# Softmax steps listed at other tiles, and additions right behind their products, in a fused window-sum and max-out kernel

## The chip, the cores and the metric

The kernel runs on one core of one Trainium2 chip. The metric is the time of one execution on the device, in microseconds; of several executions the median is given.

## What is computed

The reference has two parts. The first takes, for each position, a softmax over seven taps and sums the seven most recent rows of `x` with it, per head (8 heads of 24 columns; 8 sequences of 4160 positions):

```python
w = weight_gen - np.max(weight_gen, axis=-1, keepdims=True)
w = np.exp(w)
w = w / (np.sum(w, axis=-1, keepdims=True) + 1e-09)
...
out = np.einsum('bshk,bskhg->bshg', w, x_unf)
```

The second part takes the 33280 rows of 192 values that come out and applies two matrices of 192 x 1024, the larger of the two results, and a matrix of 1024 x 192:

```python
h1 = x @ w1
h2 = x @ w2
g = np.maximum(h1, h2)
return (g @ w_out).astype(np.float32)
```

Inputs and output are float32.

## The kernel before

**Layout.** A partition holds 260 consecutive positions. They are cut into 17 batches: 16 of 16 positions and one of 4. A batch is done in halves of 8 positions (quarters of 4 in the first two batches). In the second part a *tile* is 1/8 of the hidden units for the 8 positions of one half (1024 tokens), so there are as many tiles as positions, 260: batch `b` needs its first half at tile 16b and its second at tile 16b+8.

**Per half on VectorE.** `mul` (L164, the product itself at L173) multiplies the seven shifted copies of `x` with the weights. `adds` (L179) adds the seven products in three steps (L189, L195, L198); the last writes `y_t`. Between these, in the argument `beside`, stand pieces of other batches' softmax: `shift` (L144, three pieces), which subtracts the logarithm of the sum from the exponents of the next batch, and `red` (L135, two pieces), which sums the exponentials of a batch further on. All batches share one product tile `m_t`.

**Per batch on ScalarE.** The softmax has three steps there: `exp_sum` (L125, L127) takes the exponentials to be summed, `ln` (L141) the logarithm of the sums, and `weights` (L150, L158) the exponentials of the shifted exponents, per half; these are the weights that `mul` reads. So for batch `c` the order is `exp_sum`, `red`, `ln`, `shift`, `weights`, `mul`, `adds`, with the engine changing at nearly every step.

**Transposes.** SyncE issues a DMA transpose of each finished half of `y_t` into `yt` (L207), in one queue with the stores of the results (L383). `transpose` also lets GpSimd wait for the landing by a one-column copy (L215) and then issue the loads of `x` (L115) and of `weight_gen` (L105) of later batches.

**TensorE and its other engine.** Since max(a, b) = a + relu(b - a), TensorE computes `hd` = x(w2 - w1) (L275), ScalarE applies relu into `rd_t` (L285), and TensorE adds the rest: `op_ps` from `yt` and `w10` = w1 w_out (L327), then from `rd_t` and `wo` (L315). ScalarE copies the results out (L371). This goes by *groups* of three tiles (two before tile 16). In each group `hidden` (L434) lists: the first matmuls of the group's first tiles, the results of earlier tiles (first halves), the relu of the first tiles, the group's last tile, its relu, the second halves of the results, and the copies out. A group computes two results or four. `OUTS` fixes which; from tile 58 on they alternate, before that two groups of two results often follow one another.

**Where the softmax steps stand.** Each engine works through its queue in the order in which the program lists the instructions; nothing is reordered. In a group with two results the softmax steps of ScalarE are listed after the copies out, in a group with four between the relu of the first two tiles and that of the last one (`beside`). Which steps those are is decided by the table `due` (L677 to L687): for each batch and step a tile number. `softmax_steps` (L690) takes what has become due in the tiles of the group; a long step (`weights`, `exp_sum`) that becomes due in a group with four results is put off to the next group, if the group with two results just before it had a long step. `extra` (L703) lists VectorE's work and the transposes by the tile's place `s` in its batch.

Of the kernel before, what the change touches and what calls it, by code (L numbers as in the profile page):

```python
# [17 lines left out]
def _sub(base: bass.AP, off: int, dims):  # L18
    ap = [list(base.ap[0])] + [[int(s), int(c)] for s, c in dims]
    return dataclasses.replace(base, offset=base.offset + off, ap=ap)  # L20
# [3 lines left out]
def kernel(  # L24
# [25 lines left out]
    NB = len(BATCHES)  # L50


    def pieces(b):
        n = BATCHES[b][1]
        at, done = [], 0
        for w in (4, 4, 4, 4) if b < 2 else (8, 8) if n == 16 else (n,):
            at.append((done, w))
            done += w
        return at
# [65 lines left out]
    def exp_sum(b):  # L125
        e_ts[b] = pe_.tile([P, BATCHES[b][1] * WGC], FP32, name="e_t", tag="e")
        nc.scalar.activation(out=e_ts[b], in_=wg_ts[b], func=AF.Exp)  # L127
# [7 lines left out]
    def red(b, i=0, of=1):  # L135
        if i == 0:
            s_ts[b] = psm.tile([P, BATCHES[b][1] * H], FP32, name="sum_t", tag="sum")
        hs, at, ap = part(b, i, of)
        nc.vector.reduce_sum(out=s_ts[b][:, hs], in_=_sub(e_ts[b], at, ap), axis=AX.X)  # L139

    def ln(b):  # L141
        nc.scalar.activation(out=s_ts[b], in_=s_ts[b], func=AF.Ln)  # L142

    def shift(b, i=0, of=1):  # L144
        hs, at, ap = part(b, i, of)
        w_t = _sub(wg_ts[b], at, ap)
        nc.vector.tensor_tensor(out=w_t, in0=w_t, in1=_sub(s_ts[b], hs.start, [[1, hs.stop - hs.start], [0, K]]),  # L147
                                op=ALU.subtract)

    def weights(b, o):  # L150

        w = dict(pieces(b))[o]
        if b not in en_ts:
            en_ts[b] = pen.tile([P, 16 * WGC * 2], BF16, name="en_t", tag="en")
        J = 2 if w == 4 and b < 2 else 1
        N = w * H // J
        for j in range(J):
            nc.scalar.activation(  # L158
                out=_sub(en_ts[b], (o * WGC + j * N * K) * 2, [[2 * N, K], [2, N], [1, 2]]),
                in_=_sub(wg_ts[b], (o * H + j * N) * K, [[1, K], [K, N], [0, 2]]), func=AF.Exp,  # L160
            )


    def mul(b, o):  # L164

        n = dict(pieces(b))[o]
        if n == 4 and b < 2:
            m_out = _sub(m_t, K * o * D, [[64, 2], [P, K * 6], [1, 64]])
            x_in = _sub(xb_ts[b], o * D, [[2 * D, 2], [D, K], [1, 2 * D]])
        else:  # L170
            m_out = m_t[:, K * o * D:K * (o + n) * D]
            x_in = _sub(xb_ts[b], o * D, [[D, K], [1, n * D]])
        nc.vector.tensor_tensor(  # L173
            out=m_out, in0=x_in,
            in1=_sub(en_ts[b], o * WGC * 2, [[2, K * n * H], [0, G // 2], [1, 2]]),
            op=ALU.mult,
        )

    def adds(b, o, first=False, beside=lambda i, of: None):  # L179


        w = dict(pieces(b))[o]
        n = w * D

        def taps(at, step, cnt):
            return _sub(m_t, K * o * D + at * n, [[step * n, cnt], [1, w * D]])

        beside(0, 3)
        nc.vector.tensor_tensor(out=taps(0, 1, 3), in0=taps(0, 1, 3), in1=taps(3, 1, 3), op=ALU.add)  # L189
        if first:  # L190
            return
        beside(1, 3)
        if b not in y_ts:
            y_ts[b] = py.tile([P, 16 * D], BF16, name="y_t", tag="y")
        nc.vector.tensor_tensor(out=taps(0, 2, 2), in0=taps(0, 2, 2), in1=taps(1, 5, 2), op=ALU.add)  # L195
        beside(2, 3)

        nc.vector.tensor_tensor(  # L198
            out=_sub(y_ts[b], o * D, [[64, 2], [P, 3 * w // 2], [1, 64]]),
            in0=taps(0, 1, 1), in1=taps(2, 1, 1), op=ALU.add,  # L200
        )

    def transpose(u):

        b, o, n = UNITS[u]
        yt = pyt.tile([P, 8 // 2 * 3 * P], BF16, name="yt", tag="yt")
        nc.sync.dma_start_transpose(  # L207
            out=yt[:, 0:n // 2 * 3 * P].rearrange("p (b t) -> p b t", t=P),
            in_=y_ts[b][:, o * D:(o + n) * D],
        )  # L210
        yt_ts[u] = yt
        while held:
            held.pop(0)()

        nc.gpsimd.tensor_copy(out=gate, in_=yt[:, 0:1])  # L215
        c = b + 1 if o == 0 else b + 2
        if o == 8 and c < NB:
            load_x(c, 0, min(8, BATCHES[c][1]))
        if o == 0 and c < NB and BATCHES[c][1] > 8:
            load_x(c, 8, BATCHES[c][1] - 8)  # L220
        if o == 0 and b + 3 < NB:
            load_wg(b + 3, nc.gpsimd)
# [179 lines left out]
    OUTS, c = [[], [], []], 0  # L402
# [274 lines left out]
    due = {}  # L677
    for c in range(3, NB):
        soon = c < 5
        parts_ = [(16 * (c - 2) + (8 if soon else 12), True, lambda c=c: weights(c, 0))]  # L680
        if 8 in dict(pieces(c)):
            parts_.append((16 * (c - 2) + (14 if soon else 17), True, lambda c=c: weights(c, 8)))
        if c > 3:
            parts_.append((16 * (c - 2) + (0 if c < 10 else 2 if c < 14 else 4), False, lambda c=c: ln(c)))
            parts_.append((16 * (c - 3) + (4 if c < 6 else 8), True, lambda c=c: exp_sum(c)))
        for t, *step in parts_:
            due.setdefault(t, []).append(step)  # L687
    waiting, long_in_two = [], [False]
# [14 lines left out]
    def extra(t):  # L703

        u, k = TILES[t]
        b, o, n = UNITS[u]
        s = o + k

        if s == 0 and b + 1 < NB:
            mul(b + 1, 0)  # L710
        if s == 5 and b + 1 < NB:

            c = b + 1
            adds(c, 0, beside=lambda i, of: shift(c + 1, i, of) if c + 1 < NB else None)
        if s == 8 and b + 2 < NB:
            mul(b + 1, 8)
        if s == 13 and b + 2 < NB:
            adds(b + 1, 8, beside=lambda i, of: red(b + 3, i, 2) if b + 3 < NB and i < 2 else None)
        if k == n // 4 - 1 and 7 < u + 1 < NU:
            transpose(u + 1)  # L720

    def steps(g, tiles):

        if tiles:
            softmax_steps(g)
        for t in tiles:
            extra(t)
# [47 lines left out]
```

## Time and profile before

| | us |
|---|---|
| median of 6 runs | 420.38 |
| lowest, highest | 419.48, 422.0 |
| the profiled execution | 419.53 |
| its span, first to last instruction | 417.7 |
| busy: TensorE matmuls, VectorE, ScalarE, GpSimd | 396.4, 377.4, 359.3, 84.6 |
| one `mul` of a half (L173, 128x10752) | 5.75 |
| the three additions (L189, L195, L198) of a half | 2.55, 1.75, 0.95 |
| one `weights` of a half or `exp_sum` of a batch on ScalarE | 1.04, 0.95 |
| one `ln` | 0.33 |
| DMA transpose, issue to landing: least, median, most | 3.6, 3.7, 8.1 |

A profile line of the timeline reads: start, length, engine, line of the kernel, operation, what it writes and reads, number of instructions merged; in brackets the time that the engine stood idle before it, and who ended that. A line of the waits reads: who waited, for whom, microseconds in total, number of times, the longest. A matmul's end in these rows is modelled and overlaps the next, so the pace of TensorE is read from the starts. The granted clock of TensorE is 0.997 of full speed over the span.

### The profile page before, as it was taken

The numbers are of one execution on the slowest core, as the hardware profiler recorded it, in microseconds if no ns is written. First come the engines' busy times: TensorE is split into PE (matmuls) and PEld (weight loads), VectorE is DVE, ScalarE is ACT, GpSimd is POOL, SyncE is SP. The second block draws the span as 40 slices with busy tenths as digits, with TensorE's granted clock in tenths as the row PEclk, the third lists the DMA queues.
The fourth block names the chain that finished last, engine by engine and source line by source line (L and its number), as shares of the span: only waits on it lengthen the run. The fifth ranks groups of instructions, "written<-read, shape, count | busy, mean of one in ns | idle before, by whom it ended". The sixth has DMA issues, their size and how long they took to land.

```text
span 417.7 us, 16033 instructions
## 1 busy us (share of the span) xinstructions
PE 396.4 (95%) x7369; PEld 320.5 (77%) x7369; DVE 377.4 (90%) x218; ACT 359.3 (86%) x424; POOL 84.6 (20%) x102
## 2 busy tenths in 40 slices
PE   7769899989999999899999999999999999999995
PEld 7668799767777777677787777877777777777795
DVE  5999999799989989999999999999999999999100
ACT  5888998789988999788999899999898998987871
POOL 1510101452313142011222122112121221121000
PEclk9999999999999999999999999999999999999998
DMA  8965425679864954786497677569759737742613
GB/s 246 262 159 165 107 78 79 153 135 248 169 134 80 260 134 93 226 206 137 78 264 180 85 234 175 122 140 224 157 121 218 182 66 215 189 88 78 210 53 139
DMA packets 60242, 65.68 MB, mean 157 GB/s; under 512 B 47601, under 2 KB 48497, under 8 KB 60176
## 3 DMA queue, kind: packets, MB, share of 16 engines
q1 hardware_dynamic: 51904, 40.47, 35.8%
q0 software_dynamic: 8128, 24.11, 28.5%
q8 instruction: 57, 0.93, 0.9%
q14 instruction: 9, 0.07, 0.1%
q10 hardware_dynamic: 144, 0.10, 0.1%
HBM read 35.96 MB, written 25.56 MB: 147 GB/s over the span
## 4 chain that ended last, share of the span: by engine, by line
PE 56%; DVE 23%; ACT 11%; issue 5%; DMA 3%; SPq 1%; ACTq 0%; DVEq 0%
PE op_ps L315 26%; PE hd L275 25%; DVE m_t L173 11%; ACT rd_t L285 6%; PE op_ps L327 5%; DVE m_t L189 5%; DVE m_t L195 3%; ACT en_t L158 2%; DMA ws1T<-in_moe_w_dram 2%; DVE sum_t L139 1%; DMA yt<-y_t 1%; DVE y_t L198 1%; DVE wg_t L147 1%; ACT o_t L371 1%; ACT yt L246 1%
## 5 line engine op out<-in xcount | busy, mean ns | idle before, releaser
L285 ACT ACTIVATE rd_t<-hd 128x1024 bf16<-128x1024 f32 (+1 forms) x206 | 234.4, 1186 | 29.0 <-PE hd L275 27.7
L315 PE MATMUL op_ps<-wo,rd_t 64*128 64x192 bf16 x4160 | 210.5, 243 | 0.2
L315 PEld LDWEIGHTS <-rd_t 64*128 64x128 bf16 x4160 | 180.3, 94 | 16.1 <-ACTq L348 0.9
L173 DVE TENSOR_TENSOR m_t<-xb_t,en_t 128x10752 bf16<-128x10752 bf16 (+1 forms) x37 | 187.5, 5071 | 3.6 <-ACT en_t L158 3.5
L275 PE MATMUL hd<-yt,wd 64*128 64x512 bf16 (+1 forms) x1584 | 187.5, 360 | 3.0 <-ACT rd_t L285 2.3
L275 PEld LDWEIGHTS <-wd 64*128 64x128 bf16 x1776 | 94.2, 94 | 46.6 <-issue 5.7
L215 POOL CAST gate<-yt 128x1 f32<-128x1 bf16 x29 | 48.6, 1676 | 270.8 <-DMA yt<-y_t 270.8
L189 DVE TENSOR_TENSOR m_t<-m_t 128x4608 bf16<-128x4608 bf16 (+1 forms) x34 | 79.5, 2339 | 0.1
L371 ACT COPY o_t<-op_ps 128x384 f32<-128x384 f32 (+1 forms) x99 | 57.0, 586 | 12.4 <-PE op_ps L315 12.3
L327 PE MATMUL op_ps<-w,yt 64*128 64x192 bf16 x780 | 55.4, 243 | 5.2 <-ACT w L628 1.8
L327 PEld LDWEIGHTS <-yt 64*128 64x128 bf16 x780 | 38.3, 94 | 22.3 <-issue 7.2
L195 DVE TENSOR_TENSOR m_t<-m_t 128x3072 bf16<-128x3072 bf16 (+1 forms) x29 | 50.0, 1723 | 0.1
L158 ACT ACTIVATE en_t<-wg_t 128x896 bf16<-128x896 f32 (+2 forms) x45 | 34.9, 816 | 0.1
L198 DVE TENSOR_TENSOR y_t<-m_t 128x1536 bf16<-128x1536 bf16 (+1 forms) x29 | 27.3, 941 | 0.5
L147 DVE TENSOR_TENSOR wg_t<-wg_t,sum_t 128x280 f32<-128x280 f32 (+4 forms) x45 | 22.0, 489 | 3.0 <-ACT sum_t L142 3.0
L361 DVE COPY o_t<-op_ps 128x192 f32<-128x192 f32 x1 | 0.4, 358 | 25.5 <-ACT o_t L361 25.5
L115 POOL DMA_DIRECT2D xb_t<-in_x_dram x32 | 17.3, 540 | 23.8 <-DVE m_t L173 15.8
L139 DVE TENSOR_REDUCE sum_t<-e_t 128x64 f32<-128x448 f32 (+2 forms) x30 | 19.5, 650 | 2.6 <-ACT e_t L127 2.6
L127 ACT ACTIVATE e_t<-wg_t 128x896 f32<-128x896 f32 (+1 forms) x17 | 15.9, 936 | 4.2 <-DMA wg_t<-in_weight_gen_dram 4.2
L285 ACT ACTIVATE rd_t<-hdp 128x1024 bf16<-128x1024 f32 x16 | 15.9, 1028 | 1.2 <-PE hdp L275 1.0
L275 PE MATMUL hdp<-yt,wd 64*128 64x256 bf16 x192 | 13.1, 269 | 2.2 <-ACT yt L246 1.1
L590 PE MATMUL warm<-ident 128*128 128x128 bf16 x129 | 8.8, 238 | 3.0 <-DVE ident L529 3.0
(45 smaller groups left out, 79.5 us busy)
## 6 DMA issues: line engine op xcount, KB each, us to landing
out_dram<-o_t SPq DMA_DIRECT2D x28, 768.0 KB, 5.1
xb_t<-in_x_dram POOLq DMA_DIRECT2D x28, 384.0 KB, 5.0
wg_t<-in_weight_gen_dram POOLq DMA_DIRECT2D x14, 448.0 KB, 6.1
xb_t<-xb_t POOLq DMA_DIRECT2D x16, 288.0 KB, 5.2
out_dram<-o_t SPq DMA_DIRECT2D x8, 384.0 KB, 2.7
wg_t<-in_weight_gen_dram SPq DMA_DIRECT2D x2, 448.0 KB, 5.4
xs<-in_x_dram SPq DMA_DIRECT2D x2, 384.0 KB, 6.4
xb_t<-in_x_dram POOLq DMA_DIRECT2D x1, 768.0 KB, 7.2
```

The source lines that it names most:

```text
L147: nc.vector.tensor_tensor(out=w_t, in0=w_t, in1=_sub(s_ts[b], hs.start, [[1, hs.stop - hs.start], [0, K]]), op=ALU.subtract)
L158: nc.scalar.activation(out=_sub(en_ts[b], (o * WGC + j * N * K) * 2, [[2 * N, K], [2, N], [1, 2]]), in_=_sub(wg_ts[b], (o * H + j * N) * K ...
L173: nc.vector.tensor_tensor(out=m_out, in0=x_in, in1=_sub(en_ts[b], o * WGC * 2, [[2, K * n * H], [0, G // 2], [1, 2]]), op=ALU.mult,)
L189: nc.vector.tensor_tensor(out=taps(0, 1, 3), in0=taps(0, 1, 3), in1=taps(3, 1, 3), op=ALU.add)
L195: nc.vector.tensor_tensor(out=taps(0, 2, 2), in0=taps(0, 2, 2), in1=taps(1, 5, 2), op=ALU.add)
L198: nc.vector.tensor_tensor(out=_sub(y_ts[b], o * D, [[64, 2], [P, 3 * w // 2], [1, 64]]), in0=taps(0, 1, 1), in1=taps(2, 1, 1), op=ALU.add,)
L215: nc.gpsimd.tensor_copy(out=gate, in_=yt[:, 0:1])
L275: nc.tensor.matmul(hid_out(t, f, j), lhsT=wd[half(j), s * F + f * P:s * F + (f + 1) * P], rhs=_sub(yt_ts[u][half(j), :], (s + j) % 3 * P, ...
L285: nc.scalar.activation(out=rd[:, k * 1024:(k + n) * 1024], in_=hd[:, at:at + n * 1024], func=AF.Relu)
L315: return nc.tensor.matmul(op_out(c), lhsT=rd[half(r), k * 1024 + at:k * 1024 + at + P], rhs=wo[half(r), f * D:(f + 1) * D], start=False, s ...
L327: nc.tensor.matmul(op_out(c + j), lhsT=yt_ts[u][half(j), (3 * i + (s + j) % 3) * P:(3 * i + (s + j) % 3 + 1) * P], rhs=w10[half(j), s * D: ...
L371: nc.scalar.copy(out=_sub(o, c % 24 * D, [[D, len(qs)], [h * D, 2], [1, D]]), in_=_sub(tile_, at + (qs[0] - p) * D, [[D, len(qs)], [512, 2 ...
```

## The change

The tile numbers in the table `due` are changed, and with them the place of each softmax step of ScalarE:

- `weights` of the first half, from batch 5: two tiles earlier; of the second half: two tiles earlier,
- `ln`: batch 4 two tiles earlier; batches 8 and 9 two tiles later, batches 11 to 13 two tiles later; the others stay,
- `exp_sum`: batch 5 three tiles later, batches 6 to 16 one tile earlier.

Since a group takes three tiles, and long steps can be put off, a step moves by a whole number of groups: some do not move, and some that keep their tile number do. Of those that move: `weights` of batch 4 (first half) goes from the group of tiles 40-42 to 43-45, `exp_sum` of batch 5 from 34-36 to 37-39, `ln` of batch 4 from 31-33 to 28-30, `weights` of batch 6 (first half) from 79-81 to 73-75, `ln` of batch 8 from 94-96 to 97-99, `weights` of batch 16 from 235-237 to 232-234. Both halves of `weights` stand in one group for batches 6, 9, 12 and 15 before, and for batches 5, 8, 11 and 14 after.

In addition the three additions of a half, with their `beside` pieces, are listed at the tile of their product for the first batches (`later` is 0 up to b = 3), and five tiles after it as until now for the rest.

```diff
-        parts_ = [(16 * (c - 2) + (8 if soon else 12), True, lambda c=c: weights(c, 0))]
+        parts_ = [(16 * (c - 2) + (8 if soon else 10), True, lambda c=c: weights(c, 0))]
         if 8 in dict(pieces(c)):
-            parts_.append((16 * (c - 2) + (14 if soon else 17), True, lambda c=c: weights(c, 8)))
+            parts_.append((16 * (c - 2) + (14 if soon else 15), True, lambda c=c: weights(c, 8)))
         if c > 3:
-            parts_.append((16 * (c - 2) + (0 if c < 10 else 2 if c < 14 else 4), False, lambda c=c: ln(c)))
-            parts_.append((16 * (c - 3) + (4 if c < 6 else 8), True, lambda c=c: exp_sum(c)))
+            ln_at = -2 if c == 4 else 0 if c < 8 else 2 if c < 11 else 4
+            parts_.append((16 * (c - 2) + ln_at, False, lambda c=c: ln(c)))
+            parts_.append((16 * (c - 3) + (4 if c == 4 else 7), True, lambda c=c: exp_sum(c)))
...
-        if s == 5 and b + 1 < NB:
+        later = 0 if b < 4 else 5
+        if s == later and b + 1 < NB:
 
             c = b + 1
             adds(c, 0, beside=lambda i, of: shift(c + 1, i, of) if c + 1 < NB else None)
         if s == 8 and b + 2 < NB:
             mul(b + 1, 8)
-        if s == 13 and b + 2 < NB:
+        if s == 8 + later and b + 2 < NB:
             adds(b + 1, 8, beside=lambda i, of: red(b + 3, i, 2) if b + 3 < NB and i < 2 else None)
```

## The prediction

> **Names.** Groups go by their tiles ("group 43-45"); a wide group computes four results, a narrow one two. W(c,o) is `weights`, L(c) `ln`, E(c) `exp_sum` (ScalarE); M(c,o) `mul`, S(c) the three `shift` pieces, R(c) the two `red` pieces (VectorE). All times are us of the profiled execution; "before" is the kernel as profiled.
>
> **What bounds the kernel now.** I read the page's busy times first, then the waits in total, then the timeline at each TensorE wait.
>
> ```profile
> PE 396.4 (95%) x7369; PEld 320.5 (77%) x7369; DVE 377.4 (90%) x218; ACT 359.3 (86%) x424; POOL 84.6 (20%) x102
> ```
> ```profile
> ACT sum_t L142 <- DVE sum_t L139: 5.3, 4, 1.8
> ...
> DVE m_t L173 <- ACT en_t L158: 3.5, 3, 2.1
> ...
> DVE wg_t L147 <- ACT sum_t L142: 3.0, 3, 2.2
> ...
> PE hd L275 <- ACT rd_t L285: 2.3, 2, 1.8
> ```
>
> Three engines are nearly full, so I took the pace of two of them from the timeline. TensorE: from a group's first L327 matmul to the next group's it is 5.08 after a wide and 3.56 after a narrow group, so 8.64 per six tiles or 23.0 per batch of 16. VectorE: M(10,0) starts at 242.44 and M(11,0) at 266.11, 23.67 per batch. VectorE is slower by 0.6 per batch, so a head start is eaten, and in the second half TensorE waits for transposed tiles. VectorE's own waits on ScalarE after tile 16 are three: 2.21 for L(4) (at 76.8), 1.08 for W(5,0), 2.14 for W(6,0): 5.43.
>
> TensorE's losses against 5.08/3.56 after tile 28: 0.60 before group 37-39 (W(3,8) and L(4) between two narrow groups), 2.22 before 40-42, 0.26 after the W, L, W of group 79-81, 1.32 at L(8), 0.28, 0.27 and 0.19 after the double W of 127-129, 175-177 and 223-225, 0.69 at tile 184 and 0.27 at tile 200 for a transpose, 0.07 at 224. Sum 6.2: the most that the change can touch.
>
> **The change, part by part.** Only ScalarE's order differs: VectorE, SyncE, GpSimd and TensorE keep theirs, since the additions already follow their products there, so listing those earlier costs and gains nothing. No DMA moves.
>
> *E(5), from after group 34-36 to after 37-39.* It now waits 1.72 for its load, and the relus behind it end late: the waits blame ScalarE for TensorE's 1.80.
>
> ```profile
> 78.37 3.33 SPq L207 DMA_TRANSPOSE yt<-y_t  x1
> ...
> 86.59 4.40 POOL L215 CAST gate<-yt 128x1 f32<-128x1 bf16 x1 [8.70 <-DMA yt<-y_t]
> 86.67 1.47 PE L275 MATMUL hd<-yt,wd 64*128 64x512 bf16 x12 [1.80 <-ACT rd_t L285]
> ```
>
> But tile 40 also needs this transpose, which lands 8.1 after its issue, at 86.47 (GpSimd's copy that waits for it starts at 86.59); the relu ended at 86.50. Two causes end together; the change removes one. The transpose is issued behind a store (77.93, 384 KB, 7.5 to landing), as before. [...] By the waits row alone I would book -2.4, the stall of this group and most of the one ahead; by landing and rule 86.67 becomes 86.51: **-0.16**. I take that, the landing being the nearer row; a later landing, from other traffic, no row here shows, and it would cost what it is late.
>
> *W(4,0), put off.* E(5) is now the long step of a narrow group, so W(4,0) of wide 40-42 goes to after narrow 43-45. (a) ScalarE has 0.2 to spare between narrow groups. The nearest row is the 0.65 that W(3,8) with L(4) cost; L takes 0.20 of ScalarE's queue (78.69 to 78.89): **+0.45**, ends 0 and 0.65. Queued behind it are the relus of 46-48, then the first matmuls of 49-51. (b) VectorE: with L(4) in 28-30 (R(4) ends 68.5, slot about 71.9) its 2.21 goes and M(3,8) starts at 82.99. M(4,0) would follow at 94.84, but W(4,0) starts 0.2 ahead of group 46-48's first L327 (96.59-0.16=96.43), and a product starts 0.89 after that L327 (121.87 against 120.98). So M(4,0) starts at 97.32, 0.27 later than before: the 2.21 is lost in a new wait of 2.5. M(5,0) waits for W(5,0) in the same place as before: 120.98-0.16+0.45+0.89 = 122.16. M(6,0) finds W(6,0) done (now after 73-75) and starts 23.66 later, 145.82 against 147.77. **VectorE: -1.95** from there. Its inputs keep pace: the closest are L(11), 0.6 ahead of S(11), L(8) and L(12), 0.7 to 1.0; if that cover went, VectorE loses what is missing.
>
> *TensorE from tile 61.* Double W after 61-63 and L(6) in wide 64-66: +0.28, as after 127-129. Triple of 79-81 gone: -0.26. L(8) from wide 94-96 to after 97-99, where R(8) is long done: -1.32. Doubles after 109-111 with L(9) +0.28, at 127 gone -0.28, after 157-159 without an L in the wide group +0.08 (ends 0 and 0.28; 0.28 less L's 0.20), at 175 gone -0.27. With -0.16+0.45 that makes -1.20. The transpose for tile 184 lands 1.95 earlier (293.2, wanted 293.4): -0.69, so -1.89. At tile 200 TensorE would be 2.16 ahead, but its transpose only 1.95: -1.95; the double after 205-207 hides in that wait. Double of 223-225 gone: -0.19. **-2.14** at group 232-234.
>
> E in wide groups (E(7), E(10), E(13), E(16)) I cost at nothing: E(8) in 88-90 left the 5.08 as it is, because ScalarE idles 0.5 there; without that idle each would cost up to 0.3, and none can gain, since nobody waits for an E. The W that move earlier (single ones go at nothing too: narrow groups before wide ones have carried one each) find their S done: the closest is W(15,0), 2.4 after its piece. The L that move carry only 0.20 of queue.
>
> *W(16,0), from after 235-237 into wide 232-234.* This is the step that decides. W needs S; with four tiles in batch 16 it needs the last piece.
>
> ```profile
> 366.17 0.43 PE L327 MATMUL op_ps<-w,yt 64*128 64x192 bf16 x6
> ...
> 366.45 1.88 ACT L285 ACTIVATE rd_t<-hd 128x2048 bf16<-128x2048 f32 x1 [0.52 <-PE hd L275]
> ...
> 370.13 0.27 DVE L147 TENSOR_TENSOR wg_t<-wg_t,sum_t 128x112 f32<-128x112 f32 x1
> ...
> 371.25 0.43 PE L327 MATMUL op_ps<-w,yt 64*128 64x192 bf16 x6
> ```
>
> The slot is 2.1 after the group's first L327: 366.17-2.14+2.1 = 366.1. S(16) ends at 370.40-1.95 = 368.45. ScalarE stands 2.3 with the group's last relu and its result copies behind W, and the next group's results need the bank those copies free. L(8) shows the same picture and its price:
>
> ```profile
> 168.90 0.31 ACT L142 ACTIVATE sum_t<-sum_t 128x128 f32<-128x128 f32 x1 [1.84 <-DVE sum_t L139]
> 169.11 1.01 ACT L285 ACTIVATE rd_t<-hd 128x1024 bf16<-128x1024 f32 x1
> ...
> 170.86 0.42 PE L327 MATMUL op_ps<-w,yt 64*128 64x192 bf16 x6 [1.19 <-ACT o_t L371]
> ```
>
> From late relu to the next results 1.75, here 1.82 (two copies, 0.86 against 0.79). So 368.45+0.05 until W starts, +0.52 for half a W, +1.82 = 370.84 against 371.25; the next group takes 3.51: **-0.46**. The last steps follow TensorE unchanged: 419.53-0.46 = 419.1. The profiled run lies 0.85 under the median, so I take the difference to it: 420.38-0.46 = **419.9**.
>
> **Rivals.** *A: ScalarE alone held tile 40* (the waits row speaks for it; the landing against). Group 40-42 starts 2.4 earlier, M(5,0) follows, VectorE is 4.35 ahead, W(16,0) ends the gain at -4.35+1.49 = -2.9 (1.49 being -0.46+1.95): 417.5. 15%.
> *B: W(16,0) costs nothing*, the relu behind it or the bank not being needed so soon: -2.14, 418.2. The L(8) rows speak against. 12%.
> *C, slower: W(16,0) waits at its full price*, VectorE not having gained, as when M(5,0) comes 1.95 later, held by the transpose for tile 40 landing later or by more than 0.45 at W(4,0). Then S(16) ends at 370.4 and the end is +1.49, 421.9; it is over 0.3% slower once VectorE gains less than 0.2. Against: 1.95 is several times the 0.2 uncertainty of (a). 10%.
> The forecast, small gain eaten at tile 232: 63%, own range 419.3 to 420.6 from the ends above.
>
> **Numbers.** A measurement here tells 0.3% (1.26) from no change: faster below 419.1, slower above 421.6. A, B and a little of the forecast give faster 0.28; C and a little give slower 0.11; same 0.61. The range reaches to A and most of the way to C: 417.5 to 421.3.
>
> **What would show it.** A wait of ScalarE's L158 for VectorE's L147 near 366, some 2.3 long, and a late L327 after it; none for L142 near 168. M(4,0) waiting 2.5 for L158, M(6,0) not at all. TensorE still starting tile 40 near 86.5; if it starts near 84, A is right. Wrong altogether if VectorE meets other waits on L142 or if stores make transposes land late (3.7 is the median, 8.1 the longest).

## The result and the profile after

The changed kernel takes 421.22 us (median of 28 runs, 416.87 to 423.66); the kernel before, run beside it, 421.06 (63 runs, 417.69 to 422.96). The ratio is 0.9996 with a 95% interval of 0.9982 to 1.001: no difference that can be measured, as forecast. The ratio leaves out one slow execution of after (423.66), so it is not exactly the ratio of the two medians. The median lies outside the narrow range of the forecast (419.3 to 420.6) and only 0.08 inside the wide one (417.5 to 421.3); part of that is that before itself has 421.06 here and had 420.38 when the forecast was made. The profiled execution of after took 420.13 us (span 418.3), 0.60 more than that of before, where the forecast was 0.46 less. So "no difference" was right, but one term of the sum was not, and in the profiles it turned the sign.

The first row of the page of after: nothing became busier or less busy by more than 0.8, apart from GpSimd (84.6 before), whose 29 one-column copies took 46.0 in all and 48.6 before.

```profile
PE 396.7 (95%) x7369; PEld 321.3 (77%) x7369; DVE 377.3 (90%) x218; ACT 359.2 (86%) x424; POOL 81.9 (20%) x102
```

The waits of after, in total (who waited for whom: total, times, longest):

```profile
DVE m_t L173 <- ACT en_t L158: 4.8, 3, 3.4
ACT sum_t L142 <- DVE sum_t L139: 3.5, 3, 1.3
PE hd L275 <- DMA yt<-y_t: 3.1, 1, 3.1
...
ACT en_t L158 <- DVE wg_t L147: 2.3, 1, 2.3
PE op_ps L327 <- ACT o_t L371: 1.9, 3, 1.5
...
DVE wg_t L147 <- ACT sum_t L142: 0.8, 2, 0.4
```

Against the rows of before: L(4) and L(8) hold nobody any more (3.0 became 0.8 on VectorE, 5.3 became 3.5 on ScalarE), but in their place stand a longer wait of a product for its weights, a wait of 3.1 for one transpose, and 2.3 of W(16,0) for its shift. The timeline of after at the transpose for tile 40:

```profile
71.17 5.75 DVE L173 TENSOR_TENSOR m_t<-xb_t,en_t 128x10752 bf16<-128x10752 bf16 x1
71.53 5.44 POOL L215 CAST gate<-yt 128x1 f32<-128x1 bf16 x1 [24.84 <-DMA yt<-y_t]
76.91 0.54 POOL L115 DMA_DIRECT2D xb_t<-in_x_dram  x1
...
78.45 4.20 SPq L207 DMA_TRANSPOSE yt<-y_t  x1
...
85.45 0.98 ACT L127 ACTIVATE e_t<-wg_t 128x896 f32<-128x896 f32 x1
...
87.53 1.25 POOL L215 CAST gate<-yt 128x1 f32<-128x1 bf16 x1 [9.55 <-DMA yt<-y_t]
87.55 1.47 PE L275 MATMUL hd<-yt,wd 64*128 64x512 bf16 x12 [3.07 <-DMA yt<-y_t]
```

E(5) stands behind the relus of group 37-39 now and waits for nothing; ScalarE is out of the way, as rival A wanted. Group 40-42 still starts late, and later than before: the transpose landed at 87.41 (GpSimd's copy that waits for it starts 0.12 later), 0.94 after that of before. And the end of the timeline, at W(16,0):

```profile
365.08 0.43 PE L327 MATMUL op_ps<-w,yt 64*128 64x192 bf16 x6
...
365.36 1.88 ACT L285 ACTIVATE rd_t<-hd 128x2048 bf16<-128x2048 f32 x1 [0.33 <-PE hd L275]
...
369.25 0.27 DVE L147 TENSOR_TENSOR wg_t<-wg_t,sum_t 128x112 f32<-128x112 f32 x1
...
369.55 0.62 ACT L158 ACTIVATE en_t<-wg_t 128x448 bf16<-128x448 f32 x1 [2.32 <-DVE wg_t L147]
...
371.88 0.42 PE L327 MATMUL op_ps<-w,yt 64*128 64x192 bf16 x6 [1.54 <-ACT o_t L371]
```

From 365.08 to 371.88 it is 6.80 where 5.08 is the pace: 1.72 lost, 1.68 forecast.

TensorE's offset, after less before, by the first L327 of a group, shows where the time came from and went. A step is what the distance from one group to the next gained or lost against before; "forecast" is the prediction's running sum.

| where | step measured | step forecast | offset then | forecast |
|---|---|---|---|---|
| up to 37-39 (L(4) gone from it) | -0.11 | 0 | -0.11 | 0 |
| group 40-42 (transpose) | +0.98 | -0.16 | +0.88 | -0.16 |
| 46-48 to 49-51 (E(5), W(4,0)) | +0.47 | +0.45 | +1.35 | +0.29 |
| 64-66 (double W(5)) | +0.37, 0.05 of it given back | +0.28 | +1.67 | +0.57 |
| 82-84 (triple gone) | -0.31 | -0.26 | +1.36 | +0.31 |
| 97-99 (L(8)) | -1.37 | -1.32 | +0.04 | -1.01 |
| 112-114, 130-132, 160-162, 178-180 (doubles) | -0.07 | -0.19 | -0.03 | -1.20 |
| tile 184 (transpose) | -0.70 | -0.69 | -0.73 | -1.89 |
| tile 200 and the double of 223-225 | -0.36 | -0.25 | -1.09 | -2.14 |
| 235-237 (W(16,0)) | +1.72 | +1.68 | +0.63 | -0.46 |
| end | | | +0.58 | -0.46 |

The row of tile 200 hides a misreading of the forecast. It let the double after 205-207 vanish in the wait at tile 200, but that wait stands ahead of the double and not behind it. The double cost 0.20, of which 0.05 came back; the rest of the row (tiles 200 and 224, double of 223-225 gone) gained 0.51 for 0.25.

### The profile page after: what moved, and what is told of

Read it like the earlier page. It is cut to its first block, busy times and chain, and to the rows that moved or that the text cites. A ratio compares the mean times of both kernels' runs of the same rounds, so it can differ in the third digit from the quotient of the medians.

```text
span 418.3 us, 16029 instructions
## 1 busy us (share of the span) xinstructions
PE 396.7 (95%) x7369; PEld 321.3 (77%) x7369; DVE 377.3 (90%) x218; ACT 359.2 (86%) x424; POOL 81.9 (20%) x102
## 4 chain that ended last, share of the span: by engine, by line
PE 64%; DVE 14%; ACT 11%; DMA 5%; issue 4%; SPq 1%; DVEq 0%; ACTq 0%
PE op_ps L315 30%; PE hd L275 28%; DVE m_t L173 8%; ACT rd_t L285 6%; PE op_ps L327 6%; DVE m_t L189 3%; DMA yt<-y_t 2%; ACT en_t L158 2%; DVE m_t L195 2%; DMA ws1T<-in_moe_w_dram 2%; DMA out_dram<-o_t 1%; ACT o_t L371 1%; DVE wg_t L147 1%; ACT yt L246 1%; DVE sum_t L139 1%
## 5 line engine op out<-in xcount | busy, mean ns | idle before, releaser
L275 PE MATMUL hd<-yt,wd 64*128 64x512 bf16 (+1 forms) x1584 | 187.3, 360 | 3.8 <-DMA yt<-y_t 3.1
L275 PEld LDWEIGHTS <-wd 64*128 64x128 bf16 x1776 | 94.2, 94 | 47.0 <-issue 6.8
L215 POOL CAST gate<-yt 128x1 f32<-128x1 bf16 x29 | 46.0, 1587 | 272.0 <-DMA yt<-y_t 272.0
L327 PE MATMUL op_ps<-w,yt 64*128 64x192 bf16 x780 | 55.5, 243 | 5.5 <-ACT o_t L371 1.9
L327 PEld LDWEIGHTS <-yt 64*128 64x128 bf16 x780 | 38.3, 94 | 22.7 <-issue 7.5
L275 PE MATMUL hdp<-yt,wd 64*128 64x256 bf16 x192 | 13.1, 269 | 2.0 <-ACT yt L246 1.1
```

The costliest lines, as they stand in the source:

```text
L275: nc.tensor.matmul(hid_out(t, f, j), lhsT=wd[half(j), s * F + f * P:s * F + (f + 1) * P], rhs=_sub(yt_ts[u][half(j), :], (s + j) % 3 * P, ...
L327: nc.tensor.matmul(op_out(c + j), lhsT=yt_ts[u][half(j), (3 * i + (s + j) % 3) * P:(3 * i + (s + j) % 3 + 1) * P], rhs=w10[half(j), s * D: ...
```

## The experiments

All were timed beside the kernel before, in four comparisons (medians of before 420.38 to 420.96). Runs 3, 5, 6 and 9 have 6 executions each, the others 12 to 22. The letters and offsets are those of the prediction.

**1. The additions and L(4) where they were.** With `later = 5` alone L(4) would stand ahead of the R(4) that it reads, which rides on those additions; so the two are undone together.

```diff
-            ln_at = -2 if c == 4 else 0 if c < 8 else 2 if c < 11 else 4
+            ln_at = 0 if c < 8 else 2 if c < 11 else 4
...
-        later = 0 if b < 4 else 5
+        later = 5
```

> The changed kernel with the additions listed five tiles after their product everywhere, and ln of batch 4 back in the group of tiles 31-33 (it can only stand earlier when the red pieces of batch 4 do, which ride on those additions). Theory: VectorE again waits 2.2 us for ln of batch 4 at 76.8 us, M(3,8) starts at 85.2 instead of 82.99, but M(4,0) waits for W(4,0) in both, so it starts at 98.4 as in the changed kernel; the time is that of the changed kernel within 0.3 us, ratio to before 1.000. Rival: the earlier ln is what the change lives on, and without it VectorE is 2.2 us later to the end: 1.005.

Measured: 420.47, ratio 0.9996 (0.9975 to 1.0017). VectorE waits 2.2 for L(4) again and M(3,8) starts at 85.15 (82.99 in after); M(4,0) waits all the same for W(4,0), until 99.90 (98.36 in after; TensorE lost 1.7 in this profile at a clock of 0.50, see run 11). What the earlier listing saves there is lost at the next product. "Costs and gains nothing" holds for the time, but not quite for the mechanism: it is what lets L(4) stand earlier.

**2. W(16,0) back after group 235-237.**

```diff
-        parts_ = [(16 * (c - 2) + (8 if soon else 10), True, lambda c=c: weights(c, 0))]
+        parts_ = [(16 * (c - 2) + (8 if soon else 12 if c == NB - 1 else 10), True, lambda c=c: weights(c, 0))]
```

> The changed kernel with only weights of batch 16 back in the narrow group 235-237. Theory: ScalarE's wait of 2.3 us for the last shift piece of batch 16 is gone, the step from group 232-234 to 235-237 is 5.08 us again instead of 6.80, and nothing after it takes the place: 1.7 us less than the changed kernel, ratio to before 0.996. Rival: the transposes are the limit there (VectorE is slower than TensorE), and the 1.7 us comes back as a wait for yt at tiles 236 to 256: ratio 1.000.

Measured: 419.51, ratio 0.9954 (0.9935 to 0.9973). The step from 232-234 to 235-237 is 5.08 and no other wait takes its place. So this one step cost more than the 1.09 by which TensorE was ahead when it came to it. The profiled execution (415.18, the fastest of the 20) is worth reading for another reason. Its timeline, GpSimd beside VectorE, SyncE and TensorE:

```profile
70.75 0.36 POOL L215 CAST gate<-yt 128x1 f32<-128x1 bf16 x1 [24.25 <-DMA yt<-y_t]
70.98 5.75 DVE L173 TENSOR_TENSOR m_t<-xb_t,en_t 128x10752 bf16<-128x10752 bf16 x1
71.20 0.54 POOL L115 DMA_DIRECT2D xb_t<-in_x_dram  x1
...
78.25 1.49 SPq L207 DMA_TRANSPOSE yt<-y_t  x1
...
83.91 4.68 POOL L215 CAST gate<-yt 128x1 f32<-128x1 bf16 x1 [11.64 <-DMA yt<-y_t]
84.15 1.47 PE L275 MATMUL hd<-yt,wd 64*128 64x512 bf16 x12
```

The transpose for tile 32 landed at 70.62 and not at 71.40: just ahead of the product M(3,0), not just behind its start. So GpSimd's one-column copy took 0.36 and not 5.44, the loads went out 5.7 earlier, the transpose for tile 40, issued at 78.25, landed at 83.78, and TensorE did not wait for it at all.

**3. The transpose for tile 40 ahead of the stores.** The stores of tiles 24 to 31 (units 6 and 7 in the code; the expectations of this run and of run 5 name neighbouring ones) are handed on behind the next transpose, as those of later tiles are already.

```diff
-            if 8 <= u < NU - 3:
+            if 6 <= u < NU - 3:
```

> The changed kernel with the two stores of units 5 and 6 held back until the transpose for tile 40 has been issued, as the kernel does from unit 8 on. Theory: the transpose is issued when its half is ready (about 71.3 us instead of 78.4), lands before 80, TensorE starts tile 40 near 84.4 instead of 87.55, and W(4,0), M(4,0), M(5,0) all follow: 3.2 us less than the changed kernel, ratio to before 0.9925. Rival (ScalarE or the loads hold tile 40, not this transpose): no change against the changed kernel, 1.000.

Measured: 416.96, ratio 0.9909 (0.9885 to 0.9933). The transpose is the second of the pair in the first row, issued at 71.16 and landed at 75.20:

```profile
67.20 5.40 SPq L207 DMA_TRANSPOSE yt<-y_t  x2
...
85.47 1.47 PE L275 MATMUL hd<-yt,wd 64*128 64x512 bf16 x12
```

TensorE doesn't wait (step 3.56), and the rest follows. In the changed kernel the landing alone holds tile 40.

**4. The same in the kernel before.**

```diff
-            if 8 <= u < NU - 3:
+            if 6 <= u < NU - 3:
```

> The kernel before with the same two stores held back. Theory of two causes: the transpose lands before 80, but exp_sum of batch 5 still stands in ScalarE's queue until its load lands near 83.8 and the relus behind it end at 86.5, so TensorE still starts tile 40 near 86.6; M(5,0) and M(6,0) hang on it as before: 0 to 0.3 us less than before, ratio 0.9995. Rival 1 (the transpose alone held tile 40): 2.2 us less, 0.995. If e3 gains 3 and this one nothing, each of the two alone is hidden by the other.

Measured: 419.23, ratio 0.9958 (0.9939 to 0.9976); a miss, since I had expected next to nothing. Its timeline is as I thought:

```profile
83.52 0.95 ACT L127 ACTIVATE e_t<-wg_t 128x896 f32<-128x896 f32 x1 [1.16 <-DMA wg_t<-in_weight_gen_dram]
...
86.35 1.47 PE L275 MATMUL hd<-yt,wd 64*128 64x512 bf16 x12 [1.53 <-ACT rd_t L285]
```

The transpose has landed at 75.76, E(5) still waits for its load, and group 40-42 starts 0.32 earlier than before. Yet the median falls by 1.7. The executions show where: 10 of the 12 have a mean granted clock of 0.997 or more, against 17 of the 47 of before beside them, and among those the medians are 419.18 and 420.08, 0.9 apart. The other 0.8 goes with the larger share at the higher clock, whose cause stays open. For the 0.9 a later landing in most executions of before would account, but one profile of before cannot show that. In the profiled executions with late loads that began on time the landing ranged from 86.47 (before) to 87.41 (after), so 86.47 is the early end.

**5. Both edits that helped, on after.** W(16,0) at its old group and the stores behind the transposes.

> The changed kernel with both edits that helped: W(16,0) back after group 235-237, and the stores of tiles 24 to 39 handed on behind the transposes. My theory (each wait is its own term, and the two do not meet): the step from group 232-234 to 235-237 returns to 5.08, which takes 1.05 from the run with the stores behind the transposes alone, and no transpose after tile 184 is late; ratio to before 0.988 (416.0 us). Rival (VectorE is the bound at the end, so a wait taken from ScalarE comes back as a wait for VectorE's last products): the same as with the stores alone, 0.991.

Measured: 415.96, ratio 0.987 (0.9843 to 0.9897). The step at 235-237 is 5.08 again and the two gains add, as 0.988 had it; VectorE does not take the gain back, as 0.991 would have shown.

**6. W(4,0) and W(5,0) not put off, on top of run 5.**

```diff
-            parts_.append((16 * (c - 3) + (4 if c == 4 else 7), True, lambda c=c: exp_sum(c)))
+            parts_.append((16 * (c - 3) + (4 if c == 4 else 7), c not in (5, 6), lambda c=c: exp_sum(c)))
```

> The kernel of the run before (W(16,0) at its old group, stores behind the transposes) with E(5) and E(6) no longer counted as long steps, so that W(4,0) and W(5,0) are not put off: W(4,0) in wide group 40-42, W(5,0) in wide 58-60. My theory (each wait a term of its own): M(4,0), M(5,0) and M(6,0) no longer wait (0.27 and 1.11 in that run), VectorE is 1.4 ahead from M(6,0) on; TensorE gets back the 0.49 at 46-48, 0.37 after 64-66 and 0.45 at tile 184; the end comes 1.3 earlier, ratio 0.984 (414.6 us). Rival (a W in the wide group right after a narrow one with E has no room): the steps after 40-42 and 58-60 grow from 5.08 by 0.3 each and the ratio is 0.986 or more.

Measured: 414.86, ratio 0.986 (0.9826 to 0.9893), the fastest of all. The ratio can't tell the two theories apart, the profile can: M(4,0), M(5,0) and M(6,0) no longer wait (95.63, 119.30, 142.96); the steps are 3.56 at 46-48 (4.05 in run 5), 5.08 after 64-66 (5.45), 3.56 at tile 184 (4.01), and those after 40-42 and 58-60 grow to 5.13 and 5.14 only. Counted from group 6-7, the last L327 comes 1.45 earlier than in run 5.

**7. L(8) and L(9) alone, on before.**

```diff
-            parts_.append((16 * (c - 2) + (0 if c < 10 else 2 if c < 14 else 4), False, lambda c=c: ln(c)))
+            parts_.append((16 * (c - 2) + (0 if c < 8 else 2 if c < 14 else 4), False, lambda c=c: ln(c)))
```

> The kernel before with one edit of the change alone: L(8) and L(9) two tiles later. My theory: L(8) no longer stands in front of the relu of group 94-96, so the step to 97-99 is 5.08 (6.45 before, -1.3); but VectorE has gained nothing, its transposes for tiles 184, 200 and 224 land when they did, and TensorE waits there for as much longer: 2.0 at tile 184 in place of 0.69. At the last group the offset to before is within 0.2; ratio 1.000 (0.999 to 1.001). Rival (TensorE sets the end, each stall counts): -1.3 at the end, ratio 0.997.

Measured: 421.2, ratio 1.0015 (0.9996 to 1.0034). The step to 97-99 is 5.08, 1.37 less, and the offset to before falls from 3.58 (this execution lost 3.1 in its first groups) to 2.21. By the last group it is 3.66 again. The waits show where it went; the row of before has 0.6, once:

```profile
PE hd L275 <- DMA yt<-y_t: 3.3, 4, 1.9
```

So L(8) alone buys nothing: TensorE reaches transposes earlier that VectorE finishes when it did. The places differ from my expectation (the steps to groups 127-129, 163-165 and 223-225 rather than tile 184), the sum doesn't.

**8. W(16,0) alone, on before.**

```diff
-        parts_ = [(16 * (c - 2) + (8 if soon else 12), True, lambda c=c: weights(c, 0))]
+        parts_ = [(16 * (c - 2) + (8 if soon else 10 if c == NB - 1 else 12), True, lambda c=c: weights(c, 0))]
```

> The kernel before with one edit of the change alone: W(16,0) in wide group 232-234. My theory: W(16,0) waits for the last S(16) piece, which ends at 370.4 as before; the relu and the copies behind it free the bank 2.4 later, so the step from 232-234 to 235-237 is 6.6 (5.08 before) and the end comes 1.5 later; ratio 1.0036. Rival (nobody needs what stands behind W(16,0) so soon): 5.08 and ratio 1.000.

Measured: 422.07, ratio 1.0026 (1.0011 to 1.004). The copies behind the late relu hold the bank of the next results; 6.56 from 366.78 to 373.34, 1.5 lost:

```profile
371.01 0.62 ACT L158 ACTIVATE en_t<-wg_t 128x448 bf16<-128x448 f32 x1 [2.08 <-DVE wg_t L147]
...
373.34 0.42 PE L327 MATMUL op_ps<-w,yt 64*128 64x192 bf16 x6 [1.30 <-ACT o_t L371]
```

**9. The first load not held to GpSimd's copy, on after.**

```diff
-        nc.gpsimd.tensor_copy(out=gate, in_=yt[:, 0:1])
+        if u > 8:
+            nc.gpsimd.tensor_copy(out=gate, in_=yt[:, 0:1])
```

> The changed kernel without GpSimd's one-column copy at the first transpose (tile 32) alone, so that the loads of x(3,8) and wg(5) are no longer held to after that copy, which in the profile ran 71.5 to 76.9 beside VectorE's product M(3,8-ahead) and put the loads at 76.9 and 77.4, right ahead of the store and the transpose for tile 40. The output is unchanged. My theory (the loads, late by that copy, crowd the transpose for tile 40): they land before 75, the transpose, issued at 78.4 still, lands in under 6 us, before 84.5; group 40-42 starts near 85.5 and the runs spread as narrowly as with the stores behind the transposes; ratio 0.993 (418.0 us). Rival (the store issued just ahead alone holds the transpose): it lands at 86.5 or later, ratio 0.999 to 1.000 and the spread stays. Risk: loads that start early meet the first transpose, which has 2.5 to spare.

Measured: 418.16, ratio 0.9928 (0.9901 to 0.9956). The loads land at 54.87 and 55.81, the store stays ahead of the transpose, and the transpose, issued at 78.94, lands at 84.43 (one line is new in this kernel, so L275 is L276 here):

```profile
78.94 1.50 SPq L207 DMA_TRANSPOSE yt<-y_t  x1
...
84.85 1.47 PE L276 MATMUL hd<-yt,wd 64*128 64x512 bf16 x12
```

The issue itself takes 1.50, not 4.20. So of the lateness that run 3 takes away, the two loads are the part that decides; the store ahead alone leaves the transpose in time.

**10. The same on before.**

> The kernel before with one edit that is not of the change: no one-column copy of GpSimd at the first transpose, so that the loads of x(3,8) and wg(5) go out near 47. My theory (one late load is behind both causes at tile 40: E(5) waits for it and the transpose is crowded by it): E(5) does not wait, the transpose lands before 85, group 40-42 starts at 85.7 (87.96 before), the later waits for W(5,0) and W(6,0) move with it, and the end comes 2.2 earlier than in the profiled execution of before: 417.3, ratio 0.9915. Rival 1 (the transpose alone, as when the stores went behind it): 0.996. Rival 2 (the store ahead alone makes it late): 0.999 to 1.000.

Measured: 418.98, ratio 0.9962 (0.9946 to 0.9977), less than forecast. E(5) waits for nothing and the transpose lands 5.6 after its issue, at 86.06. TensorE is held by the relu behind E(5) alone:

```profile
86.95 1.47 PE L276 MATMUL hd<-yt,wd 64*128 64x512 bf16 x12 [0.28 <-ACT rd_t L286]
```

This execution ran 2.1 late up to group 37-39; the step to 40-42 is 3.96 (5.78 before), 1.82 less, and at the last group it is 0.35 behind before: 1.75 gained, 2.2 forecast. I had left out that E(5) between two narrow groups costs 0.40 (3.96 for 3.56) even when it waits for nothing. And the ratio forecast, 0.9915, set the profiled execution of before less 2.2 against a median that lies 1.4 above that execution; 2.2 off the median is 0.995. The late load is a common cause of both waits; by the median it is worth no more than run 4.

**11. E(5) back at its old group, on after.**

```diff
-            parts_.append((16 * (c - 3) + (4 if c == 4 else 7), True, lambda c=c: exp_sum(c)))
+            parts_.append((16 * (c - 3) + (4 if c < 6 else 7), True, lambda c=c: exp_sum(c)))
```

> The changed kernel with one part undone: E(5) back after group 34-36, which puts W(4,0) back into wide group 40-42. My theory (the transpose for tile 40 sets group 40-42 whatever ScalarE does): ScalarE waits for the load again, group 40-42 starts where the transpose lands, as in the changed kernel; what returns is the 0.47 of the step 46-48 to 49-51 and the wait of M(4,0), which falls from 3.4 to under 1.5; the end comes 0.4 to 0.6 earlier, ratio to before 0.9985 (0.997 to 1.000), unresolved by the medians. Rival (moving E(5) was what made or would make tile 40 earlier): group 40-42 starts later than the landing, by the relu behind E(5), over 0.5, and the ratio is 1.001 or more.

Measured: 420.64, ratio 0.998 (0.996 to 1.0001). The step at 46-48 is 3.56 and M(4,0) starts at 95.61, 2.75 earlier than in after, as expected, and the ratio is the one I expected; but in the profile the offset at the end is worse than in that of after (+1.5 against +0.6). Group 40-42 starts at 89.24, 2.1 after the landing at 87.14 where 1.43 is usual, and its step is 6.07. That is neither theory. The windows (stretch and its length in us; busy time and instructions of TensorE, weight loads, VectorE, ScalarE, GpSimd; granted clock; DMA share; GB/s) give the reason:

```profile
86.00:88.00 2.00, 0.72 (x7) 0.40 (x9) 2.00 (x1) 2.00 (x4) 0.73 (x1) 0.97 0.38 84
88.00:90.00 2.00, 2.00 (x18) 1.28 (x16) 2.00 (x3) 0.77 (x2) 1.96 (x3) 0.50 0.39 124
90.00:92.00 2.00, 2.00 (x38) 2.00 (x36) 2.00 (x2) 1.46 (x1) 0.00 (x0) 0.68 0.91 125
92.00:94.00 2.00, 2.00 (x44) 1.69 (x41) 2.00 (x2) 1.65 (x2) 0.00 (x0) 1.00 0.92 166
```

The granted clock is at half from about 87.8 to 91.2 (by windows of 0.4); the group comes 0.67 late after the landing and its step takes 0.99 more, 1.7 in all. Run 1's profile shows the same stretch at half after its wait of 2.88; those of before, after and run 8 don't, after waits of 1.80, 3.07 and 2.18.

**12. The wait filled with matmuls, on after.**

```diff
+        if t == 40:
+            for i in range(20):
+                nc.tensor.matmul(hid_out(t, fs[0], i % 2), lhsT=wd[half(i % 2), 0:P],
+                                 rhs=wd[half(i % 2), 0:w], start=True, stop=True, skip_group_check=True)
```

> The changed kernel with 20 matmuls added in front of the first ones of group 40-42 (on weights alone, into the bank that those overwrite; the output is unchanged): TensorE has 2.2 of work in the 3.1 in which it waits for the transpose for tile 40. Group 40-42 should start where the transpose lands, as in the changed kernel. Two profiles so far (the additions as before, and E(5) at its old group) show the granted clock at 0.50 for 3.4 right after this wait, which took about 1.6 more. My theory (the wait lets the clock drop in a part of the executions, and that is why the changed kernel's median lies above its profiled execution): with the gap filled fewer executions lose it; of those with a mean clock of 0.997 or more there are over half (6 of 28 in the changed kernel), and the median falls by 0.6 to 1.5 to a ratio of 0.996 to 0.998. Rival (the clock drops for reasons of its own): the share stays under a third and the ratio is 0.999 to 1.000.

Measured: 420.85, ratio 1.0003 (0.998 to 1.0025). The gap is filled as meant, and the granted clock is 1.00 in every stretch of 2 from 80 to 96:

```profile
85.21 2.33 PE L274 MATMUL hd<-wd 64*128 64x512 bf16 x20
87.86 1.47 PE L279 MATMUL hd<-yt,wd 64*128 64x512 bf16 x12 [0.31 <-DMA yt<-y_t]
```

Of 12 executions 7 have a mean clock of 0.997 or more, as the theory has it; but so have 11 of 17 of before, run beside it, and the median did not fall. The run decides nothing: neither theory got both its numbers.

## Why the prediction held, point by point

**The decisive step, W(16,0), was right** in place, mechanism and size: a wait of 2.3, the row named beforehand, 1.72 lost for 1.68 forecast. Run 8 shows it alone (+1.5), run 2 takes it away. Rival B falls with this. The size came out although both engines were about 1.05 later than forecast: the wait is the distance between VectorE's last `shift` piece and ScalarE's slot, and both had moved by the same.

**L(8) and tile 184 were right** (-1.37 and -0.70). In after the group behind L(8)'s old slot starts without a wait:

```profile
170.90 0.43 PE L327 MATMUL op_ps<-w,yt 64*128 64x192 bf16 x6
```

Run 7 shows that L(8)'s gain needs VectorE's: without it, it is given back at the transposes. What VectorE's gain is worth without L(8) was not run.

**W(4,0) put off was right on both engines**: +0.47 on TensorE for +0.45 (and W(3,8), now without L(4), costs the same 0.47 at group 37-39, as the forecast took the price apart), and a new wait of M(4,0), of 3.4 instead of 2.5 because TensorE was later. The timeline of after, the three products:

```profile
98.36 5.76 DVE L173 TENSOR_TENSOR m_t<-xb_t,en_t 128x10752 bf16<-128x10752 bf16 x1 [3.44 <-ACT en_t L158]
...
123.21 5.76 DVE L173 TENSOR_TENSOR m_t<-xb_t,en_t 128x10752 bf16<-128x10752 bf16 x1 [1.10 <-ACT en_t L158]
...
146.89 5.75 DVE L173 TENSOR_TENSOR m_t<-xb_t,en_t 128x10752 bf16<-128x10752 bf16 x1
```

M(6,0) waits for nothing, as forecast; but it starts 0.88 ahead of before and not 1.95.

**The doubles and the doubtful small ones** were each 0.1 too cheap at most (+0.37 less 0.05 for +0.28, +0.20 less 0.05 for +0.08), except the double after 205-207, put at nothing by the misreading above: it cost 0.15.

**The step that failed is E(5)'s: "by landing and rule 86.67 becomes 86.51: -0.16".** Its mechanism, two causes that end together, of which the change removes one, was right: ScalarE was free and TensorE waited for the transpose, so rival A falls. Its size was wrong: 86.67 became 87.55, +0.88. I took the landing of before, 8.1 after the issue, as a constant; it was 9.0. The "rule" in this term no run shows; the runs showed a landing 1.09 behind that of the store ahead in before (85.38, 86.47) and 1.19 in after (86.22, 87.41), and, with this store ahead in both, landings at 83.78 (run 2) and 87.41 (after). Everything after it follows: M(5,0) comes 0.88 after TensorE's group 64-66, so VectorE's gain shrank from 1.95 to 0.88, TensorE stood at -1.09 and not -2.14 at group 232-234, and the end is at +0.58 and not -0.46. That is rival C's mechanism at about half its strength (M(5,0) 1.05 later than forecast, for 1.95). I had named it and given it a tenth.

The later landing is not shown to be the change's doing. Run 8, whose code is that of before up to tile 231, landed it at 87.04, and run 2, which is after but for W(16,0), at 83.78. The early landing of run 2 goes with the transpose for tile 32, which landed 0.36 before VectorE started M(3,0); in after it landed 0.23 behind that start. Run 9, which sends the loads early by an edit, gets the same early landing (5.5 after the issue in both), so the loads are the cause of that. What spreads the late landings stays open: 87.14 to 87.41 in the three profiles with the change, 86.47 and 87.04 in the two without, are too few to tell chance from the change.

**And a later landing hurts both kernels.** In before it replaces E(5)'s wait, which ends at nearly the same time (run 4, run 10). Each of the two hides the other, so moving E(5) could not pay here. (With the loads early it does: the step to 40-42 is 3.56 in run 9 and 3.96 in run 10. The 0.47 of W(4,0) takes that back.) That forecast and result agree is in part luck: the profiles differ by 1.06 from the forecast, the medians less, since the profiled execution of before lies 1.5 under its median and that of after only 1.1.

**Left open:** how often the clock at half, after the wait for tile 40 (runs 1 and 11) or in the first groups (0.50 from 32 to 34 in runs 3 and 10), accounts for the spread of the runs. Beside runs 1 to 4, 17 of 47 executions of before had a mean clock of 0.997 or more and a median of 420.08, the other 30 had 421.73; one stretch at half, as in run 11, costs about that difference. In run 5 the two kinds do not differ (415.99 and 415.81), so a lower mean clock alone does not say that time was lost. Whether the wait brings the half clock on, run 12 could not show.

## What to carry over

When two waits end within 0.1 of each other, as here, price the step that removes one at nothing, and treat the other's end as a range, not as the value of one execution: a landing that crosses other transfers moved by 3.6 here between executions. Before moving a step of an in-order engine earlier, compare its slot with the time at which its input is ready; what stands behind it, and not the step itself, sets the price (1.7 for a wait of 2.3). A gain that needs another engine to follow, like L(8)'s, counts only together with that engine's own.

## What the runs showed of the hardware

A one-column copy of GpSimd took 0.36 when it started 0.23 before a product on VectorE (run 2) and 5.44 when it came 0.36 after the product's start (after), where it ended 0.04 behind the product. So it went nearly always in the fourteen profiles: of 347 such copies that started during a product of 8 positions, 338 ended within 0.06 of its end (24 of 25 in before, 26 of 26 in after). What that reached, from run 2 to after: 0.8 in the landing of one transpose (70.62, 71.40) became 5.7 in the issue of two loads (71.20, 76.91 for the first), 3.6 in the landing of the next transpose (83.78, 87.41), and the whole wait of TensorE (none, 3.07).

The granted clock fell to 0.50 for 3.4 after a wait of TensorE of 1.95 (run 11) and of 2.88 (run 1), and stayed at 1.00 after 1.80 (before), 2.18 (run 8) and 3.07 (after). The length of the wait alone does not tell these five profiles apart. In run 11 0.8 of matmuls lay between the wait of 1.95 and 0.80 of idle before it.
